# A four-layer attention kernel: which part of the output weights is copied in DRAM, and when border values are made

## The chip, the cores and the metric

The kernel runs on one core of one Trainium2 chip. The metric is device time in microseconds (us) of one execution, as the median over several runs. A core has five engines with instruction queues of their own: PE (TensorE, matrix products), DVE (VectorE), ACT (ScalarE), POOL (GpSimd) and SP (SyncE, which here only issues transfers). Transfers (DMAs) are issued from the queues of SP, POOL and ACT and are carried out by 16 DMA engines. The data are in DRAM at first; work is done in SBUF, an on-chip memory of 128 partitions, and PE writes its products to eight PSUM banks.

## The reference

Four layers, A, B, A, B, each behind a layernorm and with a residual sum. x is 2048 x 640 (bf16). Layer A is attention over segments of 32 tokens with a memory of 8 rows that each segment hands to the next, so that the 64 segments follow one another. 32 heads of 192 columns; the three input weights are 640 x 6144, the output weight Wo is 6144 x 640.

```python
def _A_ref(x, mem0, Wq, Wk, Wv, Wo, seg_len):
    ...
    for s in range(n_seg):                      # 64 segments
        xs = x[:, s * seg_len:(s + 1) * seg_len, :].copy()
        h = jnp.concatenate([mem, xs], axis=1)  # 8 + 32 rows
        q = jnp.einsum('btd,dhe->bhte', h, Wq)
        k = jnp.einsum('btd,dhe->bhte', h, Wk)
        v = jnp.einsum('btd,dhe->bhte', h, Wv)
        scores = jnp.einsum('bhqe,bhke->bhqk', q, k) * scale
        scores = jnp.where(mask[None, None], scores, -1000000000.0)
        p = _softmax(scores, axis=-1)
        o = jnp.einsum('bhqk,bhke->bhqe', p, v)
        o = jnp.einsum('bhte,hed->btd', o, Wo)
        mem = o[:, :M, :].copy()
        outs.append(o[:, M:, :])
...
x = x + _A_ref(_layernorm(x, axis=-1), A_mem0, A_Wq, A_Wk, A_Wv, A_Wo, A_seg_len)
x = x + _B_ref(_layernorm(x, axis=-1), B_wqkv, B_w_phi, B_wo)     # linear attention
x = x + _A_ref(_layernorm(x, axis=-1), A_mem0, A_Wq, A_Wk, A_Wv, A_Wo, A_seg_len)
x = x + _B_ref(_layernorm(x, axis=-1), B_wqkv, B_w_phi, B_wo)
```

Layer B is not touched by the change.

## The kernel before, in words

Layer A (`layer_A`, called for li = 0 and li = 2; these are the first and the third layer) has a prologue, `A_pre`, and a chain over the 64 segments, `A_chain`. Heads are worked in four rounds r = 0 to 3 of eight heads.

Of the 40 rows of a segment the last eight ("border" tokens) do not depend on the memory, so their keys, queries and values can be made for many segments at once. The prologue does so. `keys_and_queries(h, r)` makes keys and queries of half h of the segments for round r: 12 PSUM banks of PE work (L985, `ps_pre`), moved in turn by DVE (L94) and ACT (L96) into one of two staging buffers `sts`, which lie in the space of the output weights (`wo_mid`), and then stored by one DMA of 1.5 MB (L994, `kqb`), from POOL's queue except for the last one, which ACT's queue issues. `first_values(r)` makes the border values of the first segments (L940), stages them in `wo_end` (`vts`) and stores two of 97 KB, three for r = 0 (L261, `vb`), from POOL's queue. The round order is 3, 2, 1, 0 in the first layer, and 0, 2, 3, 1 in the third. In the first layer the order of all engines in the prologue is the order of the code (`tc.manual_schedule()`); in the third only SP's is, and a scheduler orders the others. In the chain all are by hand.

A segment in the chain runs Q, K and V projections of 32 rows for four rounds (L1154), scores (L1191, `ps_s`), softmax, the product with the values (L1204), and the product with Wo (L1263, `ps_w`). The border keys and queries come back from `kqb` by POOL's DMA (L1123) and are copied into `QK` by POOL (L1130, `extra_kq`); border values by L1134 (`extra_v`). The scores of a round wait for that copy. The rows of the first segment come as `first_rows` (L1001, SP) and are turned by DVE into `hT` at the chain's start (L1081); the rows of the first layer are normalized in the prologue and written to DRAM (`xn`, POOL, L927).

Weights: most of Wq, Wk and Wv stays in SBUF; in each segment seven pieces of 384 KB are streamed into slots (L748, SP's queue). Wo has 24 pieces (r, k) of 128 x 1280 (320 KB). Twenty stay in SBUF: rounds 1 and 2 in `wo_mid`, the pieces k = 0 and 1 of rounds 0 and 3 in `wo_own`, and k = 2 to 5 of one of these two rounds in `wo_both`, which is filled again in every segment with the other round's four pieces (L797, `load_piece`). The input has Wo by heads, while PE needs 32 columns of each of four heads on 128 partitions. `lay_out_wo` (L816) therefore copies all of Wo, DRAM to DRAM, into `wo_rows` [4, 128, 7680] with 32 DMAs of 240 KB, once, in the first layer; resident pieces are then loaded from `wo_rows` by one DMA of 320 KB each (L774, `load_wo`), in each of the two layers. `early_wo` loads ten pieces in the prologue; `late_wo` the other ten at the chain's start and in the first segment, as their place in SBUF comes free.

SP issues its DMAs in order and gives each one of eight completion signals in turn, so that an issue waits until the DMA eight before it has landed; POOL does the same with eight of its own. A DMA into a staging place waits until the stores that read it have landed.

Of the kernel before, what the change touches and what calls it, by code (L numbers as in the profile page):

```python
# [8 lines left out]
P = 128  # L9
# [9 lines left out]
OWN = 4  # L19
# [4 lines left out]
VH = 194  # L24
# [98 lines left out]
class Kernel:  # L123
# [139 lines left out]
    def kept_tokens(self, k):  # L263
        return (self.later_tokens if k else self.under[:, self.ot_at:self.ot_at + 320]).rearrange("p (b t) -> p b t", b=self.KC)

    def first_rows(self):
        return self.under[:, self.ot_at + 576:self.ot_at + 736]
# [425 lines left out]
    def factors(self):  # L693

        at, out = self.ot_at + 2 * VH + 384, []
        for n in (64, 64, 16, 16):
            out.append(self.under[:, at:at + n])
            at += n
        return out

    def layer_A(self, xn_dram, at_dram, li, x_raw=None):
# [10 lines left out]
        wov = self.A_Wo.rearrange("h d m -> (h d) m").rearrange("(q j f) m -> q f j m", j=6, f=32)  # L712
# [50 lines left out]
        early = {(2, 4), (2, 5), (1, 0), (1, 1), (1, 2), (1, 3), (0, 0), (0, 1), (0, 4), (0, 5)}  # L763

        def load_wo(r, part):
            for k in part:
# [7 lines left out]
                nc.sync.dma_start(out=into, in_=self.wo_rows[r, :, 1280 * k:1280 * k + 1280])  # L774
# [21 lines left out]
        def load_piece(into, r, c):  # L796
            self.last_load = nc.sync.dma_start(out=into[:, c:c + 1280], in_=self.wo_rows[r, :, own + c:own + c + 1280])  # L797
# [11 lines left out]
        if li == 0:  # L809
            self.wo_rows = dram.tile([4, P, 7680], BF16, name="wo_rows")  # L810

        def lay_out_wo(rs):
            for r in rs:
                for h in range(4):
                    for G in range(2):
                        nc.sync.dma_start(out=self.wo_rows[r, 32 * h:32 * h + 32, 3840 * G:3840 * G + 3840]  # L816
                                          .rearrange("f (j m) -> f j m", m=640), in_=wov[8 * r + 4 * G + h])

        def early_wo(first):
            sooner = {(0, 0), (0, 1), (2, 4), (2, 5)}  # L820
            for r in (0, 2, 1):
                load_wo(r, [k for k in range(6) if (r, k) in early and ((r, k) in sooner) == first])

        def late_wo(r, part=range(6)):
            load_wo(r, [k for k in part if (r, k) not in early])
# [10 lines left out]
    def A_pre(self, xn_dram, li, load_matrix, piece, wo_mid, wo_end, lay_out_wo, early_wo, x_raw):  # L836
# [10 lines left out]
        sts = [wo_mid[:, 6144 * i:6144 * i + 192 * SH].rearrange("p (s f) -> p s f", f=192) for i in range(2)]  # L847
        vts = [wo_end[:, 2 * VH * i:2 * VH * i + 2 * VH] for i in range(2 * NR + 1)]
# [702 lines left out]
```

## Time and profile before

| | us |
|---|---|
| median of 3 runs | 3168.8 (3167.74 to 3173.45) |
| profiled execution: its own time | 3169.9 |
| profiled execution: span from first to last instruction | 3168.0 |
| busy in the span: PE / DVE / ACT / POOL | 2993.8 / 2184.4 / 1906.3 / 1392.8 |
| first layer: chain's first projection (start) | 133.84 |
| first layer: first scores (start) | 150.95 |
| first layer: segment 1's first projection (start) | 177.74 |
| third layer: chain's first projection (start) | 1724.30 |
| third layer: segment 1's first projection (start) | 1754.49 |
| copies of Wo in DRAM: first issue, last issue | 85.93, 142.02 |

The span is what the trace shows; the execution's own time is 1.9 us longer. The lines that follow in the next section are groups of instructions (line, engine, operation, output<-input, count), waits (who waited, for whom, us in total, times, longest) or single instructions in order of time. "SPq" and "POOLq" are the queues from which a DMA is issued. A landing time is given for a DMA only where the trace holds all its completions.

### The profile page before, as it was taken

What the parts mean: (1) busy time and instruction counts of PE and PEld (TensorE: products, weight loads), DVE (VectorE), ACT (ScalarE), POOL (GpSimd) and SP (SyncE); (2) the same over time, 40 slices, a digit from 0 to 9 for tenths busy, and PEclk for the clock granted to TensorE, in tenths of its full rate; (3) what the DMA queues carried; (4) which work ended last, traced back from release to release, by engine and by line L of the source; (5) the groups of instructions that cost most, each with busy time, mean ns of one, the idle gap of its engine ahead of it and who ended that gap; (6) DMA issues with size and microseconds to landing.
All of it is one profiled execution on the core that took longest, in us unless ns stands there. A gap on an engine that the chain in (4) does not pass through costs nothing.

```text
span 3168.0 us, 141538 instructions
## 1 busy us (share of the span) xinstructions
PE 2993.8 (95%) x59586; PEld 1920.6 (61%) x59586; DVE 2184.4 (69%) x5426; ACT 1906.3 (60%) x4536; POOL 1392.8 (44%) x2872
## 2 busy tenths in 40 slices
PE   8789999999999999899999999999999999998999
PEld 7656666666666665555377566666666666665553
DVE  5467777777777777656644677777777777776565
ACT  3356666666666666646433566666666666666453
POOL 3255555555555555430122555555555555554300
PEclk9999999999999999999999999999999999999999
DMA  9977777877877877840268777777877777778300
GB/s 377 340 263 257 261 248 251 265 257 250 272 252 251 267 256 246 288 166 1 103 246 320 257 255 246 263 264 245 264 259 249 255 261 255 246 259 287 130 1 34
DMA packets 338873, 749.67 MB, mean 237 GB/s; under 512 B 68874, under 2 KB 115330, under 8 KB 335166
## 3 DMA queue, kind: packets, MB, share of 16 engines
q1 hardware_dynamic: 267998, 636.89, 58.3%
q0 software_dynamic: 69376, 100.10, 10.9%
q8 instruction: 469, 7.68, 1.0%
q10 hardware_dynamic: 864, 3.64, 0.3%
q14 instruction: 166, 1.36, 0.1%
HBM read 670.77 MB, written 78.01 MB: 236 GB/s over the span
## 4 chain that ended last, share of the span: by engine, by line
PE 76%; DVE 8%; DMA 6%; issue 5%; ACT 3%; POOL 2%; ACTq 0%; DVEq 0%; SPq 0%; POOLq 0%
PE ps_qk_k L1154 13%; PE ps_qk_q L1154 13%; PE ps_v L1154 12%; PE ps_w L1263 11%; PE ps_s L1191 6%; PE ps_pre L985 4%; PE ps_o L1204 3%; PE kv L1506 2%; DVE raws L1453 2%; ACT raws L1234 2%; DVE hT L1455 2%; PE ps_pq L517 2%; PE ps_t L1217 1%; PE ps_wo L466 1%; DVE QK L1377 1%
## 5 line engine op out<-in xcount | busy, mean ns | idle before, releaser
L1154 PEld LDWEIGHTS <-hT 128*32 128x32 bf16 x30720 | 787.1, 96 | 461.0 <-DVE hT L1455 78.7
L1174 DVE STREAM_TRANSPOSE QK<-raws 128x512 bf16<-128x512 bf16 (+1 forms) x1152 | 730.0, 642 | 219.3 <-ACT raws L1169 163.7
L1130 POOL COPY QK<-kqb 64x192 bf16<-64x192 bf16 x1024 | 349.5, 341 | 486.6 <-PE ps_s L1191 254.1
L1154 PE MATMUL ps_qk_q<-arena,hT 128*32 128x384 bf16 x10240 | 511.3, 327 | 41.4 <-DVE hT L1455 25.6
L1154 PE MATMUL ps_qk_k<-arena,hT 128*32 128x384 bf16 x10240 | 510.1, 328 | 3.0 <-ACT E L1273 1.4
L1169 ACT ACTIVATE raws<-ps_qk_k 128x512 bf16<-128x512 f32 (+1 forms) x640 | 313.5, 510 | 254.0 <-PE ps_qk_k L1154 243.5
L1234 ACT ACTIVATE raws<-ps_o,under 128x192 bf16<-128x192 f32 x1024 | 373.8, 420 | 121.9 <-DVE under L1228 102.5
L1154 PE MATMUL ps_v<-arena,hT 128*32 128x384 bf16 x8192 | 428.4, 326 | 4.0 <-issue 3.0
L1169 ACT ACTIVATE raws<-ps_qk_q 128x512 bf16<-128x512 f32 x512 | 305.7, 597 | 166.6 <-PE ps_qk_q L1154 153.1
L1134 POOL DMA_DIRECT2D Vp<-vb x512 | 257.9, 504 | 316.6 <-PE ps_t L1217 210.7
L1123 POOL DMA_DIRECT2D kqb<-kqb x512 | 292.4, 571 | 69.7 <-POOL QK L1130 59.4
L1191 PEld LDWEIGHTS <-QK 128*80 128x80 bf16 x4096 | 196.0, 121 | 184.9 <-issue 153.8
L1183 DVE CAST Vp<-ps_v 64x384 bf16<-64x384 f32 x512 | 286.3, 559 | 24.5 <-ACT Vp L1181 8.7
L1263 PE MATMUL ps_w<-arena,under 128*32 128x320 bf16 x6144 | 280.6, 300 | 9.5 <-DMA arena<-wo_rows 4.1
L1191 PE MATMUL ps_s<-QK 128*80 128x80 bf16 x4096 | 253.4, 209 | 21.8 <-POOL QK L1130 13.6
L1181 ACT ACTIVATE Vp<-ps_v 64x384 bf16<-64x384 f32 x512 | 246.4, 481 | 35.1 <-PE ps_v L1154 33.6
L1273 ACT ACTIVATE E<-ps_s 80x320 bf16<-80x320 f32 x512 | 217.7, 425 | 42.8 <-PE ps_t L1217 28.6
L985 PEld LDWEIGHTS <-arena 128*128 128x128 bf16 x1920 | 187.9, 98 | 31.0 <-issue 4.7
L1119 POOL DMA_DIRECT2D attn<-under x128 | 91.3, 713 | 262.0 <-DVE under L1115 223.5
L1112 ACT ACTIVATE raws<-ps_w 64x160 f32<-64x160 f32 x256 | 76.6, 299 | 201.1 <-DVE raws L1453 199.6
L1204 PE MATMUL ps_o<-Vp,E 80*32 80x193 bf16 x4096 | 180.3, 248 | 10.2 <-issue 5.7
L1263 PEld LDWEIGHTS <-under 128*32 128x32 bf16 x6144 | 147.2, 96 | 41.6 <-issue 9.8
(167 smaller groups left out, 4360.5 us busy)
## 6 DMA issues: line engine op xcount, KB each, us to landing
arena<-wo_rows SPq DMA_DIRECT2D x560, 320.0 KB, 4.8
arena<-in_A_Wq_dram SPq DMA_DIRECT2D x427, 384.0 KB, 4.5
arena<-in_A_Wk_dram SPq DMA_DIRECT2D x298, 384.0 KB, 5.6
arena<-in_A_Wv_dram SPq DMA_DIRECT2D x290, 384.0 KB, 5.9
kqb<-kqb POOLq DMA_DIRECT2D x512, 48.0 KB, 4.3
kqb<-arena POOLq DMA_DIRECT2D x14, 1536.0 KB, 9.7
Vp<-vb POOLq DMA_DIRECT2D x512, 24.2 KB, 3.8
otb<-otb POOLq DMA_DIRECT2D x256, 48.0 KB, 4.0
```

The source lines that it names most:

```text
L985: nc.tensor.matmul(ps[:, T * i:T * i + T], lhsT=w[b][:, P * c:P * c + P], rhs=xBT[:, b, :], start=(b == 0), stop=(b == KC - 1))
L1123: nc.gpsimd.dma_start(out=kqb[:], in_=self.kqb_d[r, :, s, :])
L1130: nc.gpsimd.tensor_copy(out=o, in_=kqb[h, :].rearrange("p (x c q) -> p x c q", c=3, q=16))
L1134: nc.gpsimd.dma_start(out=Vs[n % 2][64:80, :], in_=self.vb_d[s // 8, r].rearrange("g (t s) x f -> s (g t) (x f)", s=8)[s % 8])
L1154: last = nc.tensor.matmul(o, lhsT=hT[:, b, :], rhs=rhs, start=(i == 0), stop=(i == KC - 1), tile_position=(0, 32 * g), skip_group_check=True)
L1169: nc.scalar.activation(out=raw[:, c], in_=ps[:, c], func=ACT.Copy)
L1174: nc.vector.transpose(out=o, in_=i)
L1183: nc.vector.tensor_copy(out=o, in_=i)
L1191: nc.tensor.matmul(S[0:80, c0:c0 + 80], lhsT=KT[:, 4 * x + c, :], rhs=QT[:, 4 * x + c, :], start=(c % 2 == 0), stop=(c % 2 == 1), skip_gro ...
L1204: nc.tensor.matmul(O[G][32 * h:32 * h + 32, VH * G:VH * G + 193], lhsT=E[0:80, 80 * h + 32 * G:80 * h + 32 * G + 32], rhs=V[0:80, VH * h:V ...
L1234: nc.scalar.activation(out=out, in_=i, func=ACT.Copy, scale=rc[G])
L1263: step = nc.tensor.matmul(W[q:q + 32, 0:320], lhsT=OT[i // 6][:, i % 6 // 2, 32 * (i % 2):32 * (i % 2) + 32], rhs=rhs, start=(first and i ...
```

## The change

Only the part of Wo that is streamed (rounds 0 and 3, pieces k = 2 to 5) is still copied in DRAM, into a smaller `wo_rows` [2, 128, 5120], by 16 DMAs of 80 or 240 KB (2.62 MB instead of 7.86 MB). Resident pieces are loaded straight from the input: each of the 20 pieces in each of the two layers by two DMAs of 160 KB, whose source is a pattern of 4 heads x 32 rows x 640 columns and whose destination is 128 partitions x 640 columns.

The order of the loads changes with it. In the first layer six pieces (12 DMAs) go ahead of the copies, seven (14 DMAs) to the end of the prologue; five (r = 2) and two (r = 3) into the first segment, behind its slot loads and behind the streamed pieces. In the third layer it is seven, six, five and two. The second staging buffer `sts` moves up in `wo_mid` (to 9216), so that the pieces of round 1 lie over the first staging buffer alone, and those of round 2 with k from 1 lie over the second.

In the first layer `first_values(1)` comes before the second half's keys of round 1 and `first_values(0)` before the first half's keys of round 0; in the third layer `first_values(1)` comes before both halves of round 1. On POOL's queue of the first layer the two `vb` stores of round 1 so come ahead of the last four `xn` stores, and the three of round 0 ahead of the store of `kqb` for the first half of round 0; in the third layer four `vb` stores (rounds 3 and 1) come between the `kqb` stores of rounds 3 and 1. The staging places of the values are used more than once (nine stores in three places of each of three groups of columns, two of which are the same), the fill with ones is two pieces of 1280 columns instead of one of 3492, and the kept tokens, first rows and factors move within `under`.

```diff
@@ -261,10 +261,11 @@
         queue.dma_start(out=self.vb_d[k, r, G].rearrange("c x f -> x c f"), in_=vt)
 
     def kept_tokens(self, k):
-        return (self.later_tokens if k else self.under[:, self.ot_at:self.ot_at + 320]).rearrange("p (b t) -> p b t", b=self.KC)
+        at = self.ot_at + 320 * k
+        return self.under[:, at:at + 320].rearrange("p (b t) -> p b t", b=self.KC)
 
     def first_rows(self):
-        return self.under[:, self.ot_at + 576:self.ot_at + 736]
+        return self.under[:, self.ot_at + 640:self.ot_at + 800]
 
     def ln_rows(self, lp, xt, xn):
         m = self.ln_moments(lp, xt)
...
@@ -709,7 +710,7 @@
         self.tails_d = dram.tile([NSEG // 8, 8, 8, self.Dm], BF16, name=f"tails{li}")
         self.otb_d = dram.tile([P, NSEG, 384], BF16, name=f"otb{li}")
         wview = self.wview
-        wov = self.A_Wo.rearrange("h d m -> (h d) m").rearrange("(q j f) m -> q f j m", j=6, f=32)
+        wov = self.A_Wo.rearrange("h d m -> (h d) m").rearrange("(r g h j f) m -> r g h f j m", g=2, h=4, j=6, f=32)
         low = self.view(0, LATE)
         res, slot, slot_at = {}, {}, {}
         kept = [("V", 1, b) for b in range(1, KC)]
@@ -760,7 +761,7 @@
         for r in (0, 3):
             for i in range(12):
                 wo[r, i] = wo_own[r][:, 640 * i:640 * i + 640] if i < OWN else wo_both[:, 640 * (i - OWN):640 * (i - OWN + 1)]
-        early = {(2, 4), (2, 5), (1, 0), (1, 1), (1, 2), (1, 3), (0, 0), (0, 1), (0, 4), (0, 5)}
+        late = {(2, 1), (2, 2), (2, 3), (2, 4), (2, 5), (3, 0), (3, 1)}
 
         def load_wo(r, part):
             for k in part:
@@ -771,7 +772,9 @@
                         wo_both[:, 1280 * k - own:1280 * k + 1280 - own]
                 else:
                     into = wo_mid[:, 7680 * (r - 1) + 1280 * k:7680 * (r - 1) + 1280 * k + 1280]
-                nc.sync.dma_start(out=into, in_=self.wo_rows[r, :, 1280 * k:1280 * k + 1280])
+                j = 2 * (k % 3)
+                for i in range(2):
+                    nc.sync.dma_start(out=into[:, 640 * i:640 * i + 640], in_=wov[r, k // 3, :, :, j + i])
 
         held = []
 
@@ -794,7 +797,7 @@
                 held.append(lambda: self.keep_tails(1, low))
 
         def load_piece(into, r, c):
-            self.last_load = nc.sync.dma_start(out=into[:, c:c + 1280], in_=self.wo_rows[r, :, own + c:own + c + 1280])
+            self.last_load = nc.sync.dma_start(out=into[:, c:c + 1280], in_=self.wo_rows[r // 3, :, c:c + 1280])
             return self.last_load
 
         order_first = 3 if NSEG % 2 == 0 else 0
@@ -807,22 +810,23 @@
             return res[m, r, b] if (m, r, b) in res else slot[m, b]
 
         if li == 0:
-            self.wo_rows = dram.tile([4, P, 7680], BF16, name="wo_rows")
-
-        def lay_out_wo(rs):
-            for r in rs:
+            self.wo_rows = dram.tile([2, P, both], BF16, name="wo_rows")
+
+        def lay_out_wo():
+            for r in (0, 3):
                 for h in range(4):
-                    for G in range(2):
-                        nc.sync.dma_start(out=self.wo_rows[r, 32 * h:32 * h + 32, 3840 * G:3840 * G + 3840]
-                                          .rearrange("f (j m) -> f j m", m=640), in_=wov[8 * r + 4 * G + h])
-
-        def early_wo(first):
-            sooner = {(0, 0), (0, 1), (2, 4), (2, 5)}
-            for r in (0, 2, 1):
-                load_wo(r, [k for k in range(6) if (r, k) in early and ((r, k) in sooner) == first])
-
-        def late_wo(r, part=range(6)):
-            load_wo(r, [k for k in part if (r, k) not in early])
+                    for G, i in ((0, OWN), (1, 6)):
+                        n = 640 * (6 * G + 6 - i)
+                        nc.sync.dma_start(out=self.wo_rows[r // 3, 32 * h:32 * h + 32, 640 * (i - OWN):640 * (i - OWN) + n]
+                                          .rearrange("f (j m) -> f j m", m=640), in_=wov[r, G, h, :, i - 6 * G:6])
+
+        def early_wo(part):
+            for r, ks in part:
+                assert not late & {(r, k) for k in ks}
+                load_wo(r, ks)
+
+        def late_wo(r):
+            load_wo(r, [k for k in range(6) if (r, k) in late])
 
         self.A_pre(xn_dram, li, load_matrix, piece, wo_mid, wo_end, lay_out_wo, early_wo, x_raw)
         self.A_chain(xn_dram, at_dram, li, load_slot, piece, late_wo, load_both, wo, low)
@@ -844,9 +848,8 @@
         CB = 512 // T
         NH = NSEG // SH
         NT = T // P
-        sts = [wo_mid[:, 6144 * i:6144 * i + 192 * SH].rearrange("p (s f) -> p s f", f=192) for i in range(2)]
-        vts = [wo_end[:, 2 * VH * i:2 * VH * i + 2 * VH] for i in range(2 * NR + 1)]
-        self.later_tokens = wo_end[:, (4 * NR + 2) * VH:(4 * NR + 2) * VH + 320]
+        sts = [wo_mid[:, 9216 * i:9216 * i + 192 * SH].rearrange("p (s f) -> p s f", f=192) for i in range(2)]
+        vt_at = [c + 2 * VH * i for c in (3840, 3840, 1280) for i in range(3)]
         with ExitStack() as es:
             ps_ = es.enter_context(tc.tile_pool(name=f"A{li}_preps", reuse_waits="tile", bufs=8, space=bass.MemoryType.PSUM))
             if x_raw is not None:
@@ -854,11 +857,11 @@
                 es.enter_context(tc.manual_schedule())
             else:
                 es.enter_context(tc.manual_schedule(engines={nc.sync.engine}))
-            xT = [wo_end[:, 5120 - 1280 * i:6400 - 1280 * i] for i in range(2)]
+            xT = [wo_end[:, 2560 - 2560 * i:3840 - 2560 * i] for i in range(2)]
             xB = None
             if x_raw is None:
                 xB = [[self.view(LATE - 1280 * (i + 1), 1280) for i in range(2)],
-                      [wo_mid[:, 12288 + 640 * i:12288 + 640 * i + 640] for i in range(2)]]
+                      [wo_mid[:, 6400 + 640 * i:6400 + 640 * i + 640] for i in range(2)]]
                 xT[0] = self.next_xT[:, :]
             tasks = []
 
@@ -935,11 +938,13 @@
                 for k, G in ((0, 0), (0, 1), (1, 0))[0:2 if r else 3]:
                     ps = ps_.tile([P, 512], F32, name="ps_pre", tag="bank")
                     self.tail_values(ps, lambda b: self.kept_tokens(k)[:, b, :], r, G, piece)
-                    vt = vts[2 * NR if k else 2 * r + G]
+                    at = vt_at.pop(0)
+                    vt = wo_end[:, at:at + 2 * VH]
                     evict(out=self.two_heads(vt), in_=ps[:, 0:384].rearrange("p (e f) -> p e f", e=2))
                     self.store_values(nc.gpsimd, vt, k, r, G)
 
-            nc.vector.memset(wo_end[:, 0:(4 * NR + 2) * VH], 1.0)
+            for c in (1280, 3840):
+                nc.vector.memset(wo_end[:, c:c + 1280], 1.0)
             if x_raw is not None:
                 first = [norm_tasks(lambda x, k=k: gather(x, x_raw, 0, k, (nc.sync, nc.scalar)),
                                     lambda xn, k=k: normed.__setitem__((0, k), xn)) for k in range(NT)]
...
@@ -1014,19 +1019,18 @@
                 load_round(1)
                 load_round(0)
                 fetch_first_rows()
-                lay_out_wo((0, 2, 1))
-                early_wo(True)
-                lay_out_wo([3])
+                early_wo([(0, (0, 1, 4, 5)), (1, (5,)), (2, (0,))])
+                lay_out_wo()
                 keys_and_queries(0, 2)
                 keys_and_queries(1, 2)
                 first_values(2)
                 keys_and_queries(0, 1)
+                first_values(1)
                 keys_and_queries(1, 1)
-                first_values(1)
+                first_values(0)
                 keys_and_queries(0, 0)
-                first_values(0)
                 keys_and_queries(1, 0)
-                early_wo(False)
+                early_wo([(0, (3, 2)), (1, range(5))])
             else:
                 load_round(0)
                 rows_ready(0)
@@ -1040,17 +1044,17 @@
                 load_round(3)
                 load_round(1)
                 fetch_first_rows()
-                early_wo(True)
+                early_wo([(0, (0, 1, 2, 4, 5)), (1, (5,)), (2, (0,))])
                 keys_and_queries(1, 2)
                 first_values(2)
                 keys_and_queries(0, 3)
                 keys_and_queries(1, 3)
                 first_values(3)
                 load_round(0)
+                first_values(1)
                 keys_and_queries(0, 1)
-                first_values(1)
                 keys_and_queries(1, 1)
-                early_wo(False)
+                early_wo([(0, (3,)), (1, range(5))])
             assert not tasks
         if x_raw is None:
             self.small.close()
@@ -1321,7 +1325,6 @@
                     kqs.append(load_kqb(*turns[at]))
 
             kqs = [load_kqb(0, r) for r in rounds(0)[0:2]]
-            late_wo(0)
             extra_v(0, 0)
             extra_v(0, 1)
             extra_kq(kqs.pop(0))
@@ -1354,8 +1357,6 @@
                     store_tail(otb, s - 1, rounds(s - 1)[L])
                 turn_rows(q_or_k("Q", 0))
                 turn_rows(q_or_k("K", 0))
-                if s == 0:
-                    late_wo(3, range(OWN // 2))
                 pv = v_banks()
                 project(hT, pv, "V", 0, s, range(KC))
                 v_rows(pv, 0, "sv")
@@ -1399,6 +1400,8 @@
                             tails = self.kept_tails
                         else:
                             load_both(order[L], False)
+                    if s == 0 and n == 1:
+                        late_wo(2)
                     raw = q_or_k("K", n + 1, n + 1 == L)
                     O = attend(E, n)
                     if n != 2:
@@ -1414,9 +1417,8 @@
                         output_steps(STEPS[0])
                     pv = v_banks()
                     project(hT, pv, "V", n + 1, s, range(KC))
-                    if s == 0 and n == 1:
-                        late_wo(1)
-                        late_wo(2)
+                    if s == 0 and n == L - 1:
+                        late_wo(3)
                     osc = raw_of["Q"][:, 0:384]
                     for G in range(2):
                         scaled(osc[:, 192 * G:192 * G + 192], O, rc, G, "s")
```

More of the change, by code (lines that the diff above doesn't have):

```diff
@@ L693, in factors @@
     def factors(self):
-        at, out = self.ot_at + 2 * VH + 384, []
+        at, out = self.ot_at + 800, []
         for n in (64, 64, 16, 16):
@@ L952, in busy @@
                     for _ in range(n):
-                        nc.tensor.matmul(warm[:, :], lhsT=self.ident[:, :], rhs=wo_end[:, 0:512],
+                        nc.tensor.matmul(warm[:, :], lhsT=self.ident[:, :], rhs=wo_end[:, 3840:4352],
                                          start=True, stop=True, skip_group_check=True)
```

## The prediction

> **What bounds the kernel now.** I read the page's busy shares first, then a table of windows for the two stretches that the change touches, then PE's waits there, then the transfers. Columns of the windows: busy us of each engine, granted PE clock, DMA share, GB/s.
>
> ```profile
> span 3168.0 us, 141538 instructions
> PE 2993.8 (95%) x59586; PEld 1920.6 (61%) x59586; DVE 2184.4 (69%) x5426; ACT 1906.3 (60%) x4536; POOL 1392.8 (44%) x2872
> ...
> 134.00:178.00 44.00, 23.22 (x434) 13.31 (x430) 14.44 (x38) 12.17 (x29) 14.01 (x28) 0.77 0.86 297
> 178.00:196.00 18.00, 17.81 (x426) 11.41 (x418) 12.54 (x30) 11.33 (x28) 12.49 (x25) 0.99 0.81 271
> ...
> 1724.00:1755.00 31.00, 23.34 (x434) 13.45 (x438) 14.81 (x40) 12.67 (x30) 10.69 (x23) 0.84 0.83 297
> 1755.00:1773.00 18.00, 17.44 (x422) 11.70 (x414) 12.23 (x29) 11.30 (x27) 12.93 (x26) 0.99 0.82 271
> ```
>
> PE is the bound nearly everywhere (95%). A steady segment of layer A is 18.3 us of almost unbroken PE work. The first segment of the first layer takes 43.9 us (133.84 to 177.74), that of the third 30.2 us (1724.30 to 1754.49), with the same work on PE. So 25.6 and 11.9 us are lost there, and only there can this change act. PE's waits in the two segments name what is late:
>
> ```profile
> PE ps_s L1191 <- POOL QK L1130: 13.5, 1, 13.5
> PE ps_w L1263 <- DMA arena<-wo_rows: 4.0, 6, 1.3
> ...
> PE ps_w L1263 <- DMA arena<-wo_rows: 3.9, 5, 1.5
> PE ps_qk_q L1154 <- DMA arena<-in_A_Wq_dram: 2.9, 1, 2.9
> ```
>
> The 13.5 us end a chain on POOL (start, duration, operation, idle before):
>
> ```profile
> 135.07 0.81 POOL L261 DMA_DIRECT2D vb<-arena  x1 [7.17 <-issue]
> 142.60 0.80 POOL L261 DMA_DIRECT2D vb<-arena  x1 [6.72 <-issue]
> 143.39 1.18 POOL L1123 DMA_DIRECT2D kqb<-kqb  x2
> ...
> 150.56 0.74 POOL L1130 COPY QK<-kqb 64x192 bf16<-64x192 bf16 x2 [5.00 <-DMA kqb<-kqb]
> ```
>
> Value stores (vb) run one after the other on POOL, each issued 0.3 to 0.4 us after the last landed; the first load of keys stands behind three. The rest of both segments waits for weights: what ends it is the DMA work still queued, at share 0.9 to 1.0 from 146 to 172 us. The transfers (KB each, us to landing), and one value store of SP almost alone (2677.11 to 2679.64):
>
> ```profile
> arena<-wo_rows SPq DMA_DIRECT2D x560, 320.0 KB, 4.8
> vb<-under SPq DMA_DIRECT2D x110, 97.0 KB
> wo_rows<-in_A_Wo_dram SPq DMA_DIRECT2D x32, 240.0 KB, 8.1
> under<-xn SPq DMA_DIRECT2D x2, 40.0 KB
> ...
> DMA  1211101911111121003212225262131321111202
> ...
> q1 hardware_dynamic: 130, 0.10, 13.3%
> ```
>
> The last two lines matter most. SP's queue (q1) took 13.3% of 16 engines for that store: two engines. Its DRAM side is a pattern of 2 x 64 rows. All 128 of its packets (776 B) run two at a time in the trace's packet records, here and at 195.7 to 198.5, while the 2560 B packets of loads whose outer count is 128 run 14 to 16 at a time.
>
> **The change, part by part.**
>
> *Direct loads on few engines.* 40 resident pieces (20 in each of two layers) become 80 loads of 160 KB, each reading 4 x 32 rows of 1280 B. The nearest row in form is under<-xn (L1001), which also reads 4 x 32 rows: its 128 packets come in runs of 32 back to back, at most five under way. So I take four engines per direct load: one outer index each. A 1280 B packet of the old copies took 56 ns, so a load is 32 x 56 ns = 1.8 us long, however empty the other twelve engines are. If the four are always the same, loads do not overlap: 160 KB per 1.8 us is 91 GB/s, against 300 to 400 in these stretches. Every 16-engine transfer behind them in SP's queue has its quarter on those four, and lands after them. Bounds of a load's share of the queue: 0.45 us (its 8 packets on each of sixteen engines, or four engines that change) and 1.9 us (five per cent over the row). I take 1.8: a split that follows from the pattern alone has nothing that would move it from one load to the next, though no row shows which engines serve.
>
> [...]
>
> *First layer.* Twelve direct loads go ahead of the copies (from 86 us), 14 to the end of the prologue, 10 and 4 into the first segment. Twelve are 21.6 us on the four engines, beside their share of all else: the stretch 85 to 134 moved 17.05 MB; without 24 whole copies and four pieces (7.0 MB) and with 2.62 MB of partial copies 12.6 MB remain, 0.79 MB per engine, 35 us at 22.8 B/ns. So the four are busy until about 86+22+35 = 143 if all runs on, and POOL's stores, which use them too, land later. Of the 14, ten go into wo_mid over the staging buffer of the last border keys, so they wait for the landing of kqb(0,0); call it T0. Its issue stands behind the vb chain: T0 = 135 to 148, taken 140. From there: ten loads 18 us; seven slots of 384 KB about 1 us each; ten loads 18 us; four streamed pieces at 0.84 us; four loads 7.2 us: T0 + 56 us, up to T0 + 64 with POOL's and ACT's own traffic on the four (a 1.5 MB store alone puts 96 KB, 3.7 us, on each). The output product needs all of it before segment 1; some 3 us of cold PE work follow. Segment 1 begins at 196 to 215 instead of 177.74: +18 to +37, taken +25.
>
> *Third layer.* T0 is the landing of kqb(0,1): 1716.4 before. Four vb stores now precede it; each took 5.0 to 7.6 us there, two are new ahead of it, so T0 = 1725 to 1732. The same list follows: 1785 to 1795 instead of 1754.49, +30 to +40, taken +35 (it had less slack: only 11.9 us were lost before). The first 14 direct loads (25 us, 1677 on) lie beside PE's border work, busy to 1724; hidden, or 1 to 5 us in the slots behind them, which the range takes in.
>
> *Smaller copy.* 16 copies of 2.62 MB replace 32 of 7.86 MB. Before, the eight last ones sat in front of the loads at 138.8 to 142.6. Their removal is worth what the first rival gives; with four busy engines it buys nothing.
>
> *Values one step sooner.* In the first layer POOL now issues two vb stores ahead of four xn stores. DVE's transpose of hT waited 3.08 us for xn until 110.69; two stores at 9 to 12 us, less what their earlier issue saves, make about 5 us of it, and PE, stopped at eight PSUM banks, starts the chain at about 138 instead of 133.84. On the other side kqb(0,0) no longer has three vb stores between it and the first key load, which ended 13.5 us of idle. Bounds by these rows: -12 to +5 in its own right; here it is inside T0, so it enters the sum at nothing more.
>
> *SP's issue time.* L1001's issue took 0.64 to 0.70 us, a plain load 0.33: 80 x 0.67 - 40 x 0.33 = +40 us, at most 9 of it in one first segment, beside 25 us of transfers: hidden. Memset: 2.97 us of 3492 columns becomes two of 1280 (2.2 us): -0.8 to 0 in the start, taken 0. Streamed pieces keep 128 rows of 2560 B, at another pitch: 0, bounds +-1 us in all, as PE's idle for them in steady segments is nearly nil (9.5 us before all 6144 ps_w products, 7.9 of it in the two first segments).
>
> *Sum.* +25 +35 = +60 (48 to 77) on the profiled execution's 3169.9, which stands 1.1 over the median 3168.8: median 3228.8, about 3228. The likeliest case alone: 3205 to 3250.
>
> **The rivals.**
>
> *1. Direct loads fill sixteen engines: faster.* For it: 1280 B packets move 22.8 B/ns, only 5% under 2560 B ones, so narrow rows alone cost nothing. Then 5.2 MB less copy counts: kqb(0,0) lands at about 134.6, the first scores run at 142 instead of 150.95, and 9.3 MB still to move (7.8 of loads, a 1.5 MB store) at 297 to 340 GB/s end at 162 to 166; segment 1 at about 166, -11.7 (-7 to -16). In the third layer T0 comes 8.6 us later, cover was only 8 us: +1.4 (-1 to +6). Median about 3158. Against it: the two-at-a-time packets.
>
> *2. Four engines, but others for each load.* Eight may be under way (SP reuses eight completion lanes), so they would spread; as rival 1 with 2 to 4 us lost at the ends: -8, median 3161. Speaking for it: the records name no engine. It decides when more than eight engines' worth of packets run during a row of direct loads.
>
> *3. The moved stores alone.* Sixteen engines, but vb stores at 9 to 12 us each: the first layer gains 3, the third loses 5 to 8: +3, median 3172, within the noise or just over.
>
> **How the numbers follow.** Four same engines 0.80; rival 1 0.08, rival 2 0.07, rival 3 0.05. About 0.2% (6 us) is what this kernel's times can tell from no change. Slower: 0.80 and a third of rival 3, 0.82; same: the rest of rival 3 and the low ends of 1 and 2, 0.05; faster 0.13. Range: the likeliest case from packets a fifth quicker when only four engines draw (24 loads after T0 x 0.36 = -9 us in each layer) with T0 early in both (-8), 3202, to T0 late in both (+17) with 5 us of slot delay in each layer, 3255. To leave out no more than 2 in 10 it is drawn on towards the other cases, 3180 to 3260.
>
> **What would show it.** Right: the direct loads' line has no landing time (as the rows of 2 and 4 engines above have none) and its issues in the first segment pace at about 1.8 us; DMA share in 150 to 195 us near 0.3 while SP's queue is full; PE's waits there name the slots, the streamed pieces and arena<-in_A_Wo; segments from the second on unchanged at 18.3 us. Values step: DVE's hT wait at 110 us grows to 5 us or more, the 13.5 us wait shrinks. Wrong: DMA share 0.9 between 140 and 165 and segment 1 before 175 us.

## The result, and the profile after

The changed kernel took 3251.0 us (median, 3240.7 to 3257.9) against 3168.3 us before: ratio 1.0252, 95% interval 1.0237 to 1.0267, or +82.7 us. The profiled execution after spans 3250.5 us, 82.5 more than before.

Nearly all of it lies where the forecast put it. Segment 1 of the first layer begins at 210.93 us instead of 177.74 (+33.2). The third layer's chain begins at 1759.95 instead of 1724.30, 2.5 us beyond that, and its first segment takes 72.1 us instead of 30.2 (+41.9). The later segments are as before (medians of 18.2 to 18.4 us in both traces); the last 5 us are spread over what follows.

A table of windows of the kernel after, in the columns used before (busy us of PE, PEld, DVE, ACT, POOL; granted PE clock; DMA share; GB/s): the first segments of the two layers, each in two parts and with the segment behind it.

```profile
142.00:176.00 34.00, 13.49 (x256) 7.45 (x256) 9.18 (x23) 6.87 (x16) 7.74 (x21) 0.76 0.61 195
176.00:211.00 35.00, 15.56 (x178) 6.49 (x178) 5.50 (x17) 5.02 (x13) 4.67 (x10) 0.60 0.37 118
211.00:229.00 18.00, 17.62 (x397) 11.05 (x400) 11.94 (x29) 11.09 (x27) 10.77 (x22) 0.91 0.85 266
1760.00:1796.00 36.00, 13.66 (x252) 7.60 (x253) 8.66 (x21) 7.30 (x17) 7.04 (x15) 0.70 0.65 212
1796.00:1832.00 36.00, 16.07 (x174) 6.57 (x173) 5.40 (x17) 4.94 (x13) 4.69 (x10) 0.59 0.37 117
```

Read the second and the fifth line: PE is busy less than half the time and at a granted clock of 0.6, and yet the DMA engines are busy only 37%. Neither PE nor most of the DMA engines are at work. PE's waits from 98 to 212 us and from 1759 to 1833 us say what it stands still for:

```profile
PE ps_w L1267 <- DMA arena<-in_A_Wo_dram: 18.4, 13, 2.1
PE ps_qk_q L1158 <- ACT raws L1173: 10.0, 1, 10.0
PE ps_qk_q L1158 <- DMA arena<-in_A_Wq_dram: 9.8, 3, 8.9
PE ps_pre L990 <- DVE under L1087: 5.1, 1, 5.1
...
PE ps_w L1267 <- DMA arena<-in_A_Wo_dram: 18.8, 13, 2.2
PE ps_qk_q L1158 <- ACT raws L1173: 13.0, 1, 13.0
PE ps_qk_q L1158 <- DMA arena<-in_A_Wq_dram: 9.5, 3, 8.5
```

In each layer there are thirteen waits for the direct loads, nearly one for each of the fourteen that go into the first segment, and about 9 us for a streamed weight that stood behind earlier ones. The transfers from 176 to 199 us, in 40 slices (busy tenths, then GB/s), show at what rate the loads come:

```profile
DMA  2222264322233344532222222277999999832222
GB/s 107 96 107 97 93 173 161 109 98 98 93 118 114 106 136 142 128 140 93 99 89 79 98 98 100 94 145 225 341 296 289 274 287 285 218 102 98 98 102 102
```

A digit of 2 and some 98 GB/s fit four engines of sixteen (a share of 0.25). In the stretch of nines the four streamed pieces run as well: by the trace's packet records, twelve of their 2560 B packets are under way at once there (median of 192.3 to 195.8 us) beside four of the direct loads' packets, and from 198 to 200 us, with no packet of a direct load left, the rest of these pieces runs four packets at a time. In the packet records four 1280 B packets run at once in 13.1 of the 19.8 us from 178 to 198 us, and the median packet takes 55 ns. The line of the direct loads (duration of the issue: min, median, max in ns; then who waited for them) adds something that the forecast had not:

```profile
L777 SPq DMA_DIRECT2D arena<-in_A_Wo_dram x80: 527/1599/6302, 81.8 to 1819.7; - x80
...
  PE ps_w L1267: 37.2, 26
  ACT raws L1173: 29.3, 2
```

An issue takes 1.6 us in the median: SP itself is held up about as long as a load lasts. And ACT waited twice for a direct load, 29.3 us together. Its last staging store (L999) takes its completion signal from the same eight as SP's loads (in the trace it is signal 116, which SP had given to the load issued at 143.24 us; that load landed at 154.10). It could not be issued before an earlier direct load had landed, and all of ACT's work for the first segment stood behind it:

```profile
139.74 0.74 ACT L96 ACTIVATE arena<-ps_pre 128x512 bf16<-128x512 f32 x1 [1.44 <-PE ps_pre L990]
154.20 0.36 ACTq L999 DMA_DIRECT2D kqb<-arena  x1
154.83 0.60 ACT L1173 ACTIVATE raws<-ps_qk_q 128x512 bf16<-128x512 f32 x1 [14.35 <-DMA arena<-in_A_Wo_dram]
```

### The profile page after: what moved, and what is told of

Same layout as the page of the kernel before. It is cut to its first block, busy times and chain, and to the rows that moved or that the text cites. A ratio compares the mean times of both kernels' runs of the same rounds, so it can differ in the third digit from the quotient of the medians.

```text
span 3250.5 us, 141539 instructions
## 1 busy us (share of the span) xinstructions
PE 3018.9 (93%) x59552; PEld 1926.5 (59%) x59586; DVE 2184.0 (67%) x5428; ACT 1909.7 (59%) x4536; POOL 1392.7 (43%) x2872
## 4 chain that ended last, share of the span: by engine, by line
PE 71%; DVE 7%; DMA 7%; issue 4%; ACT 3%; SPq 2%; POOL 1%; DVEq 0%; POOLq 0%; ACTq 0%
PE ps_qk_k L1158 13%; PE ps_qk_q L1158 12%; PE ps_v L1158 12%; PE ps_w L1267 10%; PE ps_s L1195 6%; PE ps_o L1208 2%; PE kv L1508 2%; DMA arena<-in_A_Wo_dram 2%; PE ps_pre L990 2%; DVE raws L1455 2%; SPq L777 2%; ACT raws L1238 2%; DVE hT L1457 1%; PE ps_pq L518 1%; PE ps_wo L467 1%
## 5 line engine op out<-in xcount | busy, mean ns | idle before, releaser
L1187 DVE CAST Vp<-ps_v 64x384 bf16<-64x384 f32 x512 | 286.0, 559 | 30.9 <-ACT Vp L1185 15.2
L1267 PE MATMUL ps_w<-arena,QK 128*32 128x320 bf16 x3072 | 137.5, 303 | 44.3 <-DVE QK L1378 24.0
```

The source lines that it names most:

```text
L1187: nc.vector.tensor_copy(out=o, in_=i)
L1267: step = nc.tensor.matmul(W[q:q + 32, 0:320], lhsT=OT[i // 6][:, i % 6 // 2, 32 * (i % 2):32 * (i % 2) + 32], rhs=rhs, start=(first and i ...
```

## The experiments

**Half as many engines for each load.** If four engines, always the same, set the pace, then two should set half the pace.

```diff
                 for i in range(2):
-                    nc.sync.dma_start(out=into[:, 640 * i:640 * i + 640], in_=wov[r, k // 3, :, :, j + i])
+                    for h in (0, 2):
+                        nc.sync.dma_start(out=into[32 * h:32 * h + 64, 640 * i:640 * i + 640],
+                                          in_=wov[r, k // 3, h:h + 2, :, j + i])
```

> The changed kernel, but each direct load is split in two loads of two heads (64 rows of 1280 B, 80 KB). Theory 'same engines each time': outer count 2 gives two engines, each load still lasts 32 packets x 56 ns = 1.8 us, and there are twice as many; the 24 loads behind the last staging store become 48, +43 us in each layer, and the earlier ones add up to 20 us per layer where their slack is used up: 3335 to 3380. Theory 'engines change from load to load' or 'the bytes and rows are the cost': at most the issue time of 80 more loads, 3245 to 3270.

Measured in one run: 3385.8 us against 3170.0 before, +216, 2.6 times the change's +83 and 6 us above the range of the first theory. The same bytes cost far more. Each load reaches two engines instead of four (a digit of 1 below, where the changed kernel has 2); there are also twice as many loads, each to 64 partitions instead of 128, but a 1280 B packet still takes 55 ns in the median (236 to 249 us). The transfers from 236 to 260 us (busy tenths, GB/s) and two of PE's groups in that stretch:

```profile
DMA  1111111111111111111111399899995211111111
GB/s 49 49 47 49 49 47 49 49 47 49 47 49 49 49 47 49 49 47 49 49 47 49 68 130 363 237 307 335 346 294 162 88 49 49 51 51 51 51 49 49
```

```profile
239.05 0.45 PE L1268 MATMUL ps_w<-arena,raws 128*32 128x320 bf16 x2 [2.94 <-DMA arena<-in_A_Wo_dram]
242.44 0.45 PE L1268 MATMUL ps_w<-arena,raws 128*32 128x320 bf16 x2 [2.94 <-DMA arena<-in_A_Wo_dram]
```

49 GB/s where the changed kernel had 98, and 160 KB every 3.4 us (239.05 to 242.44) instead of every 1.7. Had the engines changed from load to load, two loads under way would have used four, and nothing would have doubled. A queue that lets only one such load run at a time, on whichever engines, would double too. The completion records of the trace exclude that. They hold sixteen completions for a streamed piece and, besides one at the issue, four for a direct load and two for a load of this run; I read them as one for each engine that took part. In the changed kernel, five direct loads had been issued and had not landed when the streamed piece of 189.13 us was issued; that piece had twelve completions by 193.66 us and its last four only from 198.23 to 199.25, as the last of the five landed (198.46). In this run the streamed piece issued at 247.70 us had fourteen completions by 252.06 and its last two at 257.11 and 257.58. So all the direct loads under way sat on the same four engines, here on the same two, while the others were free. No row of the kernel before could show this, and no record names the engines.

**Sixteen engines, one head at a time.** The resident pieces are read with an outer count of 32 instead of 4, n neighbouring pieces (up to three) in one load.

```diff
...
-                for i in range(2):
-                    nc.sync.dma_start(out=into[:, 640 * i:640 * i + 640], in_=wov[r, k // 3, :, :, j + i])
+                for h in range(4):
+                    nc.sync.dma_start(out=into[32 * h:32 * h + 32, :].rearrange("f (j m) -> f j m", m=640),
+                                      in_=wov[r, k // 3, h, :, j:j + 2 * n])
```

> The changed kernel, but the resident pieces are read one head at a time: 32 rows of up to 6 x 640 columns in one load, neighbouring pieces together, 44 loads per layer instead of 40. Packets stay 1280 B, bytes, order, staging and the early values stay as in the changed kernel; only the outer count goes from 4 to 32. Theory 'four engines, always the same': the loads fill sixteen engines, PE's waits for arena<-in_A_Wo nearly go, segment 1 of the first layer starts at 164 to 172 us instead of 210, and the time is 3150 to 3175. Theory 'narrow rows are slow': same packets, so 3240 to 3260. Theory 'the new order and the earlier values cost it': 3230 or more.

Measured: 3192.5 us, ratio 1.0068 (1.0053 to 1.0083), +22 us. Some 60 of the 83 us are gone, so the number of engines was the main part, and neither narrow rows nor the order can be. But the expectation of 3150 to 3175 missed, and so did that of 164 to 172 us for segment 1 of the first layer (184.63): this form is not free. The transfers from 1758 to 1766 us, in the third layer's first segment:

```profile
DMA  9999999999999999999999997989999899999999
GB/s 241 199 192 184 257 297 282 220 216 210 182 201 225 173 199 220 188 205 218 243 262 243 262 198 211 346 262 365 377 328 282 243 418 354 341 371 345 358 388 258
```

To 1763 us, where the loads by head run, the engines are at work all the time and move only about 220 GB/s. From 1752 to 1780 us the 1280 B packets take 103 ns on average, against 62 in the changed kernel's first segment of that layer. The next three runs ask why.

**Small loads, and 32 partitions at a time, on the kernel before.** Three ways to load the resident pieces from `wo_rows`, everything else as before: in two loads of 128 x 640, in four of 32 x 1280, and in four of 32 x (1280 n) with n neighbouring pieces together.

```diff
-                nc.sync.dma_start(out=into, in_=self.wo_rows[r, :, 1280 * k:1280 * k + 1280])
...
+                for i in range(2):
+                    nc.sync.dma_start(out=into[:, 640 * i:640 * i + 640],
+                                      in_=self.wo_rows[r, :, 1280 * k + 640 * i:1280 * k + 640 * i + 640])
...
+                for h in range(4):
+                    nc.sync.dma_start(out=into[32 * h:32 * h + 32, :],
+                                      in_=self.wo_rows[r, 32 * h:32 * h + 32, 1280 * k:1280 * k + 1280])
...
+                for h in range(4):
+                    nc.sync.dma_start(out=into[32 * h:32 * h + 32, :],
+                                      in_=self.wo_rows[r, 32 * h:32 * h + 32, 1280 * k:1280 * (k + n)])
```

> The kernel before, whole copy and all, but each resident piece is loaded from wo_rows by two loads of 128 x 640 instead of one of 128 x 1280: the changed kernel's 160 KB, its 80 loads and its 1280 B packets, on sixteen engines and 128 partitions. Theory 'the number of engines': 3165 to 3174, as before. Theory 'narrow rows or small loads': the 14 to 18 resident loads behind the staging store would take twice as long in each layer, 3185 or more.

Measured: 3181.3 us, ratio 1.0029 (1.0016 to 1.0042), +9 us. A miss on both sides: the narrow rows and twice as many loads are not quite free, but they are no 20 us. Their packets took 61 and 65 ns on average in the two first segments, 20 to 21 B/ns against 23 for the wide ones of the kernel before. Whether the 9 us come from that or from eight loads under way holding only half the bytes was not separated.

> The kernel before, but each resident piece is loaded from wo_rows by four loads of 32 partitions x 1280 columns (80 KB, 2560 B packets, outer count 32). In the run with loads by head the 1280 B packets took 92 to 104 ns instead of 56 where only 32 partitions were written at a time. Theory '32 partitions at a time take half the rate': 2560 B packets at 180 to 200 ns instead of 102, 6.4 MB per layer at some 215 GB/s, 3178 to 3195. Theory 'it came from reading the input in 1280 B rows': packets stay near 105 ns, 3166 to 3176.

Measured: 3202.9 us, ratio 1.0098 (1.0078 to 1.0118), +31 us. The time is above the range, but this run decides nothing on the rate: the median packet stayed at 102 ns, and the mean rose only to 130 to 141. Loads of 80 KB at an issue of 0.42 us each cannot bring more than 195 GB/s. From 160 to 170 us the engines' share is 0.65 at 174 GB/s and a load lands 2.0 us after its issue, so the engines had time to spare and SP's issues set the pace.

> The kernel before, but neighbouring resident pieces are loaded from wo_rows together, by four loads of 32 partitions each (for four pieces: 32 x 5120 columns, 320 KB), so that the number of loads and their bytes stay nearly as before and SP's issue time cannot bound them, which it did in the run with 80 KB loads (0.42 us each). Theory '32 partitions at a time are written at half the rate': the packets of these loads take about twice the time per byte (some 12 B/ns per engine instead of 24), 6.4 MB per layer at about 215 GB/s, 8 to 20 us more, 3178 to 3192. Theory 'the slow packets of the runs by head came from the reading side': packets at 22 to 25 B/ns, 3164 to 3176.

Measured: 3205.3 us, ratio 1.0104 (1.0075 to 1.0133), +33 us. Here the loads are large and the issue short (0.30 us), and the packets do take twice the time: 394 ns in the median for 5120 B from 160 to 172 us, 13.0 B/ns, against 104 ns for 2560 B, 24.6 B/ns, in the kernel before. The transfers from 160 to 172 us, first of this run, then of the kernel before:

```profile
DMA  7949979959989999969999989899999998999999
...
DMA packets 784, 2.50 MB, mean 209 GB/s; under 512 B 206, under 2 KB 222, under 8 KB 747
```

```profile
DMA  9999999999899999999999999999999998999999
...
DMA packets 1990, 4.61 MB, mean 385 GB/s; under 512 B 286, under 2 KB 318, under 8 KB 1989
```

The same busy share, and 209 instead of 385 GB/s. The engines are all at work, each at about half the rate of the kernel before. So the loads that wrote 32 partitions at a time were slow where they filled the queue, reading the input (about 220 GB/s in the run by heads) or `wo_rows` (209). Earlier in the same trace, among other traffic (120 to 131 us), 192 such packets took 196 ns in the median, 26 B/ns; there they were not slow. The time lost, 33 us, is more than the 8 to 20 expected. What halves the rate no run shows.

**The earlier values alone.** The kernel before, with only the three calls of `first_values` moved.

```diff
                 keys_and_queries(0, 1)
+                first_values(1)
                 keys_and_queries(1, 1)
-                first_values(1)
+                first_values(0)
                 keys_and_queries(0, 0)
-                first_values(0)
                 keys_and_queries(1, 0)
...
+                first_values(1)
                 keys_and_queries(0, 1)
-                first_values(1)
                 keys_and_queries(1, 1)
```

> The kernel before, with nothing changed but the place of the border values: round 1's and round 0's one step sooner, as in the changed kernel. My sum took them at nothing, bounds -12 to +5; the third rival at +3. The first layer's 13.5 us wait should shrink to 3 to 9 us, the hT wait grow from 3 to 5 us or more, the third layer lose 0 to 8 us: 3162 to 3176.

Measured: 3181.1 us, ratio 1.0033 (1.0021 to 1.0046), +10.5 us, and 5 us above the expected range. In its trace the first layer's segment 1 starts at 187.46 us, 9.7 late; the third layer's first segment takes 34.3 us instead of 30.2. DVE's transpose of `hT`, then PE's waits from 98 to 212 us:

```profile
120.82 0.35 DVE L1081 STREAM_TRANSPOSE hT<-under 128x160 bf16<-128x160 bf16 x1 [11.34 <-DMA xn<-ln_xn]
```

```profile
PE ps_w L1263 <- DMA arena<-wo_rows: 15.2, 8, 10.8
PE ps_pre L985 <- DVE under L1083: 7.6, 1, 7.6
```

The 13.5 us wait for POOL's key copy is indeed gone. But its place is taken by 15.2 us of waits for weights, and the two `vb` stores ahead of `xn` make DVE wait 11.3 us instead of 3.1, which stops PE for 7.6; the chain starts at 146.46 instead of 133.84. The cost is real, the gain was covered.

**The key load freed in another way.** To see whether the 13.5 us wait ever was worth anything, the three value stores ahead of it go from another queue, without touching the order of anything else.

```diff
-                    self.store_values(nc.gpsimd, vt, k, r, G)
+                    self.store_values(nc.scalar if x_raw is not None and r == 0 else nc.gpsimd, vt, k, r, G)
```

> The kernel before, but the three value stores of round 0 in the first layer go from ACT's queue instead of POOL's, so that the first load of border keys no longer stands behind them: it can be issued at 132 instead of 143 us, and the first scores run at about 140 instead of 151. If that wait set the end of the first segment: 8 to 11 us less, 3158 to 3161. If the weights still queued set it: 0 to 4 us less, 3164 to 3169.

Measured: 3167.6 us, ratio 0.9992 (0.9976 to 1.0008): no difference that these times can tell. PE's groups in the first segment with an idle of over 10 us:

```profile
156.81 0.46 PE L1263 MATMUL ps_w<-arena,under 128*32 128x320 bf16 x4 [14.25 <-DMA arena<-wo_rows]
```

The scores wait for nothing now, and PE waits 14.25 us for weights a little later. The largest wait of the kernel before, 13.5 us in one piece, was worth 8 us at most by the interval, and by the median ratio 2 to 3: the queue of weights behind it set the end.

**ACT's wait.** The last staging store goes from POOL's queue in both layers.

```diff
-                queue = nc.scalar if turn == NH * NR else nc.gpsimd
+                queue = nc.gpsimd
```

> The changed kernel, but the last staging store of the prologue goes from POOL's queue instead of ACT's. In the changed kernel ACT waited 14.4 us for a direct load before it could issue that store, and PE waited 10.0 and 13.0 us for ACT in the two first segments. Theory 'the queue of direct loads sets the end': those two waits go, PE waits for the weights instead, 3243 to 3254. Theory 'ACT's wait is on the path': up to 10 + 13 us less, 3226 to 3240.

Measured: 3251.1 us, ratio 1.0253 (1.0238 to 1.0269), as the changed kernel against the one before. PE's waits from 98 to 212 us:

```profile
PE ps_qk_q L1158 <- DMA arena<-in_A_Wq_dram: 20.5, 3, 19.6
PE ps_w L1267 <- DMA arena<-in_A_Wo_dram: 19.1, 13, 2.1
```

The 10.0 us for ACT are gone and the wait for the streamed Wq has grown from 9.8 to 20.5: segment 1 starts at 210.88 us, as with 210.93. In the third layer the 13.0 us for ACT are gone too, and the wait for Wq is 18.5 us instead of 9.5. ACT's wait was a symptom.

**Heads, with the values back in their old place.** The run by heads, with the edit of the values undone.

> The run with loads by head (3192.5 us), with the border values put back where they were before the change. If the earlier values cost what they cost alone (+10.5 to +11 us on the kernel before) and the parts add up: 3180 to 3184. If the direct loads by head still hide some of it: 3184 to 3192. If sixteen engines were all that mattered, as the first rival had it: 3155 to 3170.

Measured: 3189.1 us, ratio 1.0062 (1.0037 to 1.0087), +20 us, four runs from 3176.9 to 3197.2; the median lies in the range of the loads that hide some of it. That is not surely less than the +22 with the values moved; the 10.5 us do not add up, since here too the weights end the segment. What remains is the loads by head.

**Direct loads from POOL's queue.** The changed kernel, with `nc.gpsimd` for `nc.sync` in the direct loads.

> The changed kernel, its 80 direct loads of 160 KB unchanged (4 x 32 rows to 128 partitions), but issued from POOL's queue instead of SP's. Theory 'the same four engines are the cost': if the engines of POOL's loads change from load to load, more than four of their 1280 B packets run at a time and SP's weights no longer stand behind them; some 12 us per layer come back as a cost, since POOL's key loads and copies wait behind 26 issues of about 0.7 us: 3170 to 3215. If POOL's loads always use the same four too, or if 4 x 32 rows are slow by themselves: 3245 or more. [...]

Measured: 3278.5 us, ratio 1.0333 (1.0294 to 1.0372), slower still. The time is the one that the second theory named, but the trace does not show its reason. PE's waits from 70 to 240 us:

```profile
PE ps_s L1195 <- POOL QK L1134: 36.7, 2, 21.9
PE ps_pre L257 <- DVE arena L94: 35.7, 1, 35.7
PE ps_w L1267 <- DMA arena<-in_A_Wo_dram: 4.7, 3, 3.1
```

PE hardly waits for the direct loads any more: 9.8 us in both layers (4.7 and 5.1) instead of 37.2; the loads land 5.0 us after their issue in the median, and up to a dozen of their packets (5120 B each on this queue) run at once, where four ran on SP's queue. That fits engines that change on this queue; no record names them. But POOL's own work, the normalized rows and the key copies, stands behind the loads, for far more than the 12 us per layer that I allowed. As a test of the time it is inconclusive.

**A version for both.** The first layer by heads with the small copy, values in their old order with round 0's stored by ACT; the rest of the copy one DMA per segment in segments 8 to 31; the third layer from `wo_rows`.

```diff
+                if li:
+                    nc.sync.dma_start(out=into, in_=self.wo_rows[r, :, 1280 * k:1280 * (k + n)])
+                    continue
                 for h in range(4):
...
+                    if s >= 8 and n == L - 1 and self.rest:
+                        self.rest.pop(0)()
```

> A version for both: in the first layer resident pieces by head straight from the input, the small copy first, the border values where they were before with round 0's stored from ACT's queue; the other 5.24 MB of the copy are laid out one DMA per segment in segments 8 to 31 of the first layer, and the third layer loads whole pieces from wo_rows. The third layer should then be as before (+-2 us), the first at 0 to -8 us, as the run with values on ACT lost its 13.5 us wait to weights that here have 5 MB less in front of them: 3160 to 3172. If loads by head are as slow in the first layer as they were in the third (+9.5 to +12 us): 3172 to 3182.

Measured: 3176.8 us, ratio 1.0017 (1.0001 to 1.0034), +6 us. In its trace segment 2 of the first layer comes 1.1 us late and that of the third no later than before; 7 of the 10 us that its span is longer lie in the last layer, which neither kernel's change touches, and stay unexplained. The order of the loads and the new staging places so cost nothing in the third layer (where neighbouring pieces are loaded together here), and the saved copy buys nothing in the first, where PE waits 9.5 us for the loads by head and 9.3 us for the streamed Wq (100 to 215 us). No run was clearly faster than the kernel before.

## Why the prediction was right

The time, 3251.0, lies in the range (3180 to 3260) on the forecast's side, 23 us above the point. It is 1 us above the likeliest case's own range as the sum gives it (3205 to 3250) and inside the 3202 to 3255 that the paragraph on the numbers works out. By its steps:

- *Four engines, the same four, 1.8 us per load.* Right, and shown: 98 GB/s and a share of 0.2 in the trace, 1.7 us from load to load, the doubling with two engines, and the last four completions of the streamed piece behind them.
- *First layer, +25 (18 to 37).* Measured +33. The staging store landed at 140.60 us, as taken; from there it took 70 us to segment 1, not 59 to 67. The mis-sized term was the first ten loads. They were put at 18 us, with up to 8 more for POOL's and ACT's traffic; by the completion records the last of them landed at 172.97, 32.4 us after the store. Four earlier direct loads were in front of them until 148.29 (7.7 us), ACT's store held them up for some 3.7 us, as forecast (5.4 us between two landings, 157.51 and 162.92, instead of 1.7), and from 165 us on their packets took 82 to 98 ns instead of 55 while the 3072 B packets of the slots ran beside them. What came behind was sized well: the slots landed in 6.7 us (7 forecast), the next ten loads in 18.8 (18), the streamed pieces in 3.4 (3.4) and the last four loads in 6.7 (7.2). These terms of the forecast add up to 53.6 us, not to the 56 that it writes; and the 7.0 MB that it takes off the stretch from 85 to 134 us are 7.2, worth 0.4 us.
- *Third layer, +35 (30 to 40).* Measured +42 for the segment and 2.5 for the later chain start. T0, less the 33 us of the first layer, was 1733 instead of 1725 to 1732, since the four `vb` stores took 5.8 to 8.7 us each, and the rest took 66 us.
- *Values one step sooner, at nothing in the sum.* The place was right, the price was not: alone they cost 10.5 us, beyond the upper bound of +5. DVE's wait for `xn` became 11.3 us alone and 8.4 in the changed kernel, not 5. In the changed kernel it hardly shows, since the loads come last.
- *SP's issue time, hidden, at 0.67 us.* The size was wrong: 1.6 us in the median, against 0.54 to 0.58 for the first two of a row. I read it as the same 1.7 us per load, counted on another row, which adds nothing.
- *ACT's wait for a completion signal* was in no step. It looked like 23 us on PE and was worth none.
- *Rival 1, 3158.* Its condition can't be had by splitting the loads by heads. With all sixteen engines the time was 3192, and where its loads of 32 partitions ran, the engines moved about 220 GB/s. Its sum, 9 MB at the rate of 128-partition loads, was therefore never put to the test.
- *Rival 2* fell with the doubling and the completions. *Rival 3*, +3, measured +10.5 alone: the third layer's first segment lost 4 us, near its 5 to 8, but the first layer lost 9.7 where it had a gain of 3.

## What to carry to other kernels

Before a copy is taken out because the source can be read in place, look at the outer count of the pattern that reads in place: here 4 instead of 128 made loads of 160 KB last 1.7 us on four engines and held up everything behind them in the queue. A share of 0.2 to 0.4 on the DMA engines with a full queue was the sign of it in this profile. And a large wait is worth only the distance to the next one: 13.5 us for a key copy and 10.0 us for ACT were both taken away here, and both times the weights were waited for instead.

## What the runs showed that I had not expected

- The issue of a direct load on SP took 1.6 us in the median and up to 6.3, against 0.54 to 0.58 for the first two of a row (132.79, 133.54, 173.54 and 174.16 us) and 0.33 in the median for a streamed piece. Issues were held up before eight loads were under way: at 189.13 us five were, and the issue took 1.5 us.
- The loads that wrote 32 partitions at a time nearly halved the rate at the same busy share: 209 instead of 385 GB/s. The share of the DMA engines alone did not show it; packet times and GB/s did.
- ACT's one DMA waited 14.4 us for a DMA of SP: in the trace both have signal 116, one of the eight that SP's loads use.
